# Gated softmax and linear attention on one core: rounds ordered by head group first, and gate logits in 512-column matmuls

## The chip, the core and the metric

The kernel runs on one core of a Trainium2 chip. The metric is the device time of one execution in microseconds (us), as a median of several. A core has five engines that run side by side and meet through semaphores: TensorE (PE; its weight loads are listed as PEld), VectorE (DVE), ScalarE (ACT), GpSimd (POOL) and SyncE (SP), which issues transfers. Matrix products land in PSUM, which has eight banks of 128x512 float32; the other tiles lie in SBUF.

## What is computed

Two attention blocks read the same x, and a sigmoid gate mixes them. Cut to what matters:

```python
B, S, D, H = 1, 2048, 512, 32        # Dh = 16
g = sigmoid((x * gate_w).sum(-1, keepdims=True))
# A: softmax attention
q, k, v = split(x @ A_wqkv)           # 32 heads of 16
p = softmax(q @ k.T * Dh ** -0.5)     # 32 x 2048 x 2048
a = merge(p @ v) @ A_wo
# B: linear attention
q, k, v = split(x @ B_wqkv)
pq, pk = phi(q), phi(k)               # phi(t) = (t + 1 if t > 0 else exp(t)) + 1e-6
o = (pq @ (pk.T @ v)) / (pq @ pk.sum(0) + 1e-6)
b = merge(o) @ B_wo
out = g * a + (1 - g) * b             # bfloat16
```

The softmax part is the large one: 134 million exponentials.

## The kernel before

The program does not write its instructions down in a loop. When it is built, a scheduler in Python plays the engines' clocks with a table of costs, picks at each step the piece of work that could run next, and appends it to that engine's list. On the chip each engine then goes through its fixed list in order and waits on semaphores.

**Rounds.** The attention is cut into 32 rounds. A round has one query block of 512 (`qc`), one group of eight heads (`t8`) and one half of it, four heads (`par`). It has 16 key blocks of 128 with four heads each, so 64 tiles of 128x512 scores.

```python
NR = NQC * 8
def rinfo(r):
    qc, k = divmod(r, 8)
    return qc, k // 2, k % 2          # query block, head group, half
```

**Exp on ACT.** Three or two score tiles at a time, in PSUM banks 0 to 2 or 3 to 4:

```python
gsets = [(0, 1, 2), (3, 4)]
pe(fns, reads=rd, writes=wr2, waves=1, m="row", cols=128 * len(fns))
op(AC, lambda: nc.scalar.activation(PT[:, slot, 0:512 * n], ps[...], ACT.Exp, scale=SCALE), ...)
```

**Exp on DVE.** To relieve ACT, the scheduler may give whole key blocks of a round to DVE, from key block 15 downwards. They use the two PSUM banks 5 and 6, which the small tasks below share. The scores are moved into an integer tile (L1151), from which four passes (L1174, L1177, L1180, L1183) make three factors that are each multiplied by V:

```python
def d_claim():                        # may DVE take a block now?
    r = apos[0]
    if r >= NR or progress() < D0:    # D0 = .8: not before 0.8 of the first round
        return None
    ...
op(DV, lambda: nc.vector.tensor_scalar(Lb[...], src, S1A, S1B, op0=ALU.mult, op1=ALU.add), ...)    # L1151, 1 or 2 tiles
# chain: X = L & 0x7F | 0x3F00; E = L & 0xFF80; X = X * L; L = L + shift
```

P times V is added up for the current round in PSUM bank 7, then transposed by DVE into U (L998), and two rounds (a pair) are normalised into OT, with the gate in the factor.

**Small tasks.** Each takes bank 5 or 6, has matmuls and then an eviction on DVE, and has an earliest progress (`nb`, in rounds) and a due one:

```python
for tb in range(NTB):
    add(("V1", tb), t_v1(tb), V1D + 0.05 * (15 - tb), V1N + V1S * (15 - tb), pre=XT)   # V1D=.7, V1N=.3, V1S=.05
add(("gate",), t_gate(), GD, GN, pre=XT)                                               # GD=1.9, GN=1.5
# K of head group t8: group 1 around 0.3 to 1.3, then
add(("K", t8, t), t_kproj(t8, t), 2 * t8 - 0.9 + 0.1 * t, 2 * t8 - 1.8 + 0.2 * t, pre=XT)
add(("Q", qc, t8), t_qproj(qc, t8), due, due - 0.6, pre=XT)                            # one for two rounds
# phi(K) from 2.5 on, G from 13.2, phi(Q), den, num from 17.2 on,
add(("out", qc, q), t_out(qc, q), ..., max(17.2 + 3.0 * qc + 3.0, 8 * qc + 8.1) + 0.3 * q if qc < 3 else 31.9, ...)
```

**The gate.** All logits come from 64 matmuls of 128 columns into one bank, then sigmoid, and then 16 small copies put it into the layout that the normalisation wants:

```python
for tb in range(NTB):
    pe([mm(BK[b][:, tb:tb + 128], xT[:, cc, 128 * tb:128 * (tb + 1)], gwb[:, cc, :], ...) for cc in range(NCC)], ...)
op(AC, lambda: nc.scalar.activation(eg[:], BK[b][:, 0:NTB], ACT.Exp, scale=-1.0), ...)
...                                    # 1 + e, reciprocal, product
for j in range(4):
    for a in range(4):
        op(DV, lambda j=j, a=a: nc.vector.tensor_copy(gv[32 * j:32 * j + 32, :, a], g0[32 * a:32 * a + 32, :]), ..., cost=0.08)
```

**Fillers.** Where PE would stand, the scheduler puts in matmuls of zeros (`sb_warm`), so that PE's activity stays up.

Of the kernel before, what the change touches and what calls it, by code (L numbers as in the profile page):

```python
# [8 lines left out]
ALU = mybir.AluOpType  # L9
# [136 lines left out]
def bass_gated_mix__mha_block__linear_attn_block__prompt_kernel(  # L146
# [26 lines left out]
    with ExitStack() as es:  # L173
# [23 lines left out]
        OT = SB("OT", [128, 3, 4, 512], BF16)  # L197
# [16 lines left out]
        eg = SB("eg", [128, NTB], FP32)  # L214
        g0 = SB("g0", [128, NTB], FP32)
# [12 lines left out]
        OBT = phk[:, 0:4096].rearrange("p (s i n) -> p s i n", s=2, i=4)  # L228
# [36 lines left out]
        r_OT = [[R(f"OT{s}_{a}") for a in range(4)] for s in range(3)]  # L265
# [8 lines left out]
        r_OBT = [[R(f"OBT{s}_{b}") for b in range(4)] for s in range(2)]  # L274
# [9 lines left out]
        r_g0 = R("g0")  # L284
# [193 lines left out]
        def t_qproj(qc, t8):  # L478
            n = 4 * qc + t8
            s, st = n % 3, n % 2  # L480
            if n == 0:
                lhs, wr = (lambda cc: wA0[:, 1, cc, :]), r_wA0[1]
            else:
                lhs, wr = (lambda cc: wA[:, 0, cc, 128 * t8:128 * (t8 + 1)]), r_wA[0]
            b = yield "bank"
            yield from proj_steps(b, lhs, lambda cc: xT[:, cc, 512 * qc:512 * (qc + 1)], [r_xT[c][qc] for c in range(NCC)] + [wr])
            if n == 0:
                yield ("dve", [r_bk[b], r_maskp], [])
                for p in range(2):
                    op(DV, lambda p=p: nc.vector.tensor_scalar(QP[:, s, p, :], BK[b], maskp[:, p:p + 1], None, op0=ALU.mult),  # L490
                       reads=[r_bk[b], r_maskp], writes=[r_QP[s][p]], cost=0.69)
                yield "free"
                return
            yield ("dve", [r_bk[b]], [r_QT[st]])
            op(DV, lambda: nc.vector.tensor_copy(QT[:, st, :], BK[b]), reads=[r_bk[b]], writes=[r_QT[st]], cost=0.69)
            yield "free"
            for p in range(2):
                for j in range(4):
                    lo = 32 * j + 16 * p
                    dma(QP[lo:lo + 16, s, p, :], QT[lo:lo + 16, st, :], f"qp{s}_{p}", reads=[r_QT[st]],  # L500
                        writes=[r_QP[s][p]] if j == 0 else [], lat=2.5)
                r_QP[s][p].w = _Raw(dma_sems[f"qp{s}_{p}"][0], dma_sems[f"qp{s}_{p}"][1], SP.clock + 2.5)
                r_QP[s][p].r = {}
# [23 lines left out]
        def t_gate():  # L527
            b = yield "bank"
            for tb in range(NTB):
                yield ("pe", xt_all + [r_gwb], [r_bk[b]] if tb == 0 else [], 1.0)  # L530
                pe([mm(BK[b][:, tb:tb + 128], xT[:, cc, 128 * tb:128 * (tb + 1)], gwb[:, cc, :], start=(cc == 0), stop=(cc == NCC - 1))
                    for cc in range(NCC)], reads=xt_all + [r_gwb], writes=[r_bk[b]], waves=1.1, cols=512)
            op(AC, lambda: nc.scalar.activation(eg[:], BK[b][:, 0:NTB], ACT.Exp, scale=-1.0), reads=[r_bk[b]], writes=[r_eg], cost=0.2)
            yield "free"
            yield ("dve", [r_eg], [])
            op(DV, lambda: nc.vector.tensor_single_scalar(g1[:], eg[:], 1.0, ALU.add), reads=[r_eg], writes=[r_g1], cost=0.08)
            op(DV, lambda: nc.vector.reciprocal(g0[:], g1[:]), reads=[r_g1], writes=[r_g0], cost=0.2)
            op(DV, lambda: nc.vector.tensor_tensor(g1[:], eg[:], g0[:], ALU.mult), reads=[r_g0, r_eg], writes=[r_g1], cost=0.1)
            gv = gT[:].rearrange("p (t a) -> p t a", a=4)
            for j in range(4):  # L540
                for a in range(4):
                    op(DV, lambda j=j, a=a: nc.vector.tensor_copy(gv[32 * j:32 * j + 32, :, a], g0[32 * a:32 * a + 32, :]),  # L542
                       reads=[r_g0], writes=[r_gT], cost=0.08)
# [39 lines left out]
        def t_z():  # L583
            b = yield "bank"
            for i in range(4):
                for h in range(4):
                    yield ("pe", r_phiK + [r_const], [r_bk[b]] if i == 0 and h == 0 else [], 1.0)
                    pe([mm(BK[b][:, i:i + 128], phiK[:, tb, 128 * i:128 * (i + 1)], ones[:], start=(tb == 0), stop=(tb == NTB - 1))
                        for tb in range(4 * h, 4 * h + 4)], reads=r_phiK + [r_const], writes=[r_bk[b]], waves=1.1, cols=512)
            yield ("dve", [r_bk[b]], [])  # L590
            op(DV, lambda: nc.vector.tensor_copy(zsb[:], BK[b][:, 0:4]), reads=[r_bk[b]], writes=[r_z], cost=0.17)
            yield "free"
            for i in range(4):
                op(PO, lambda i=i: nc.gpsimd.tensor_scalar(Zsel[:, 8 * i:8 * i + 8], mask8[:], zsb[:, i:i + 1], None, op0=ALU.mult),
                   reads=[r_z, r_mask], writes=[r_Zsel], cost=0.2)
# [41 lines left out]
        def t_num(qc, q):  # L637
# [11 lines left out]
            yield "free"  # L649
            for i in range(4):  # L650
                raw = dma(OBT[:, s, i, 128 * q:128 * (q + 1)], OB[:, sl, 128 * i:128 * (i + 1)], f"obt{sl}",
                          reads=[r_OB[sl]], writes=[r_OBT[s][q]] + r_phiK[0:8] if i == 0 else [], transpose=True, lat=2.5 + i)
            r_OBT[s][q].w = _Raw(dma_sems[f"obt{sl}"][0], dma_sems[f"obt{sl}"][1], raw.t)
            r_OBT[s][q].r = {}
            for x in r_phiK[0:8]:
                x.w = r_OBT[s][q].w

        def t_out(qc, q):
            s = qc % 2
            so = qc % 3  # L660
# [3 lines left out]
            ops_ = [(OBT[:, s, i, 128 * q:128 * (q + 1)], woB[:, i, :], [r_OBT[s][q]]) for i in range(4)]  # L664
            ops_ += [(OT[:, so, a, 128 * q:128 * (q + 1)], woA[:, a, :], [r_OT[so][a]]) for a in range(4)]
            for h in range(4):
                last = qc == NQC - 1 and h == 3
                for kk in ([[6], [7]] if last else [[2 * h, 2 * h + 1]]):
                    if kk == [7]:
                        yield ("wait", ("pair", 8 * qc + 7))  # L670
# [29 lines left out]
        D0 = .8  # L700
        DR0 = 1
# [104 lines left out]
        def rinfo(r):  # L806
            qc, k = divmod(r, 8)
            return qc, k // 2, k % 2
# [25 lines left out]
        def kq_aps(r, kb, j):  # L834
            qc, t8, par = rinfo(r)
            s = (4 * qc + t8) % 3
            return (KT[32 * j:32 * j + 32, t8, 128 * kb:128 * (kb + 1)], QP[32 * j:32 * j + 32, s, par, :],
                    [r_KT[t8][kb // 4], r_QP[s][par]])
# [154 lines left out]
        def round_end(r):  # L993
            qc, t8, par = rinfo(r)
            so = qc % 3
# [9 lines left out]
        def t_norm(qc, t8):  # L1005
            so = qc % 3
# [210 lines left out]
        V1D = .7  # L1217
        V1N = .3
        V1S = .05
        K1D = .6  # L1220
        MH2 = .9
        GD = 1.9
        GN = 1.5
# [7 lines left out]
        for tb in range(NTB):  # L1231
            add(("V1", tb), t_v1(tb), V1D + 0.05 * (15 - tb), V1N + V1S * (15 - tb), pre=XT)
        add(("gate",), t_gate(), GD, GN, pre=XT)
        for t8 in range(1, 4):
            for t in range(4):
                if t8 == 1:
                    due = K1D + (0, 0.5, 0.7, 0.1)[t]
                    add(("K", t8, t), t_kproj(t8, t), due, due - 0.3, pre=XT)
                    continue
                add(("K", t8, t), t_kproj(t8, t), 2 * t8 - 0.9 + 0.1 * t, 2 * t8 - 1.8 + 0.2 * t,  # L1240
                    pre=XT)
        for q4 in range(1, 16):
            qc, t8 = divmod(q4, 4)
            due = K1D + 0.05 if q4 == 1 else 2 * q4 - 0.9
            add(("Q", qc, t8), t_qproj(qc, t8), due, due - 0.6, pre=XT)
        for tb in range(NTB):
            add(("phiK", tb), t_phik(tb), 100 + tb, 2.5 + 0.65 * tb, pre=XT)
        PK = [("phiK", tb) for tb in range(NTB)]
        add(("wq",), t_wq(), 116, 13, pre=PK)
        add(("z",), t_z(), 117, 13, pre=PK)  # L1250
        for k, cc in enumerate((2, 3, 0, 1)):
            add(("G", cc), t_g(cc), 118 + k, 13.2 + 0.8 * k, pre=PK + ([("G", 3)] if cc < 2 else [("G", 2)] if cc == 3 else []))
        GA = [("G", c) for c in range(4)]
        add(("wo",), t_wo(), 123, 16.6, pre=GA + [("z",)])
        add(("kv",), t_kv(), 124, 16.6, pre=GA)
        for qc in range(NQC):
            for i in range(4):
                add(("phiQ", qc, i), t_phiq(qc, i), 130 + 20 * qc + i, 17.2 + 3.0 * qc + 0.5 * i,
                    pre=[("wq",)] + GA + [("num", qc - 2, q) for q in range(4) if qc >= 2])
            add(("den", qc), t_den(qc), 135 + 20 * qc, 17.2 + 3.0 * qc + 2.0,  # L1260
                pre=[("phiQ", qc, i) for i in range(4)] + [("z",), ("gate",)] + [("num", qc - 1, q) for q in range(4) if qc])
            for q in range(4):
                add(("num", qc, q), t_num(qc, q), 136 + 20 * qc + q, 17.2 + 3.0 * qc + 2.1 + 0.2 * q,
                    pre=[("den", qc), ("kv",), ("K", 3, 3), ("z",)] + ([("out", qc - 2, q)] if qc >= 2 else []))
            for q in range(4):
                add(("out", qc, q), t_out(qc, q), 140 + 20 * qc + q, max(17.2 + 3.0 * qc + 3.0, 8 * qc + 8.1) + 0.3 * q if qc < 3 else 31.9,
                    pre=[("num", qc, q), ("wo",)] + ([("pair", 8 * qc + 7)] if qc < 3 else []))
# [142 lines left out]
```

The softmax here doesn't subtract the row's maximum and nothing guards it: scores larger than these inputs give would overflow.

## Time and profile before

| what | value |
|---|---|
| time, median of 3 runs | 784.76 us (782.08 to 785.05) |
| span of the profiled execution | 781.7 us |
| mean clock granted to TensorE | 0.989 |
| chain that ended last | ACT 75%, PE 15%, DVE 6%, issue 3% |
| exp of the scores on ACT (L908) | 653 instructions |
| exp blocks given to DVE (L1174) | 104 of 512 |
| evictions L1151 | 129 of two tiles, 158 of one |
| phi exp on ACT (L550) | 32, mean 772 ns |
| DVE L1151 waiting for PE | 36.5 us in 60 waits |
| ACT L908 waiting for PE | 12.5 us in 10 waits, longest 5.8 |

A page line of instruction groups names the source line, engine and operation, then what it writes and reads with shapes and the count; after the bar, busy us and the mean length of one in ns; after the next bar, the engine's idle time just before them and what ended it. Most matmuls carry L371, because one helper emits them. PE's busy time contains fillers, and matmuls are pipelined, so a busy PE need not be at its peak. The span has a start of 9.66 us before the first exp of scores and ends 8.9 us after the last one.

### The profile page before, as it was taken

Reading aid. Unit: us, or ns where it says so; the run is one execution under the profiler, and the core shown is the slowest. Engines: PE = TensorE matmul, PEld = TensorE weight load, DVE = VectorE, ACT = ScalarE, POOL = GpSimd, SP = SyncE. Lnnn points to the kernel's source line nnn. Section 1 sums busy time; section 2 is a strip of 40 time slices with the busy share of each in tenths; the row PEclk is TensorE's granted clock in tenths of the full one; section 3 lists DMA queues with packets and bytes.
Section 4 is the critical chain, followed back from the end, with each engine's and each line's share of the span. In section 5 each row is a group of like instructions: output and inputs, shape, how many; then the busy total and the mean of one; then the engine's idle time right before and its main releaser. Section 6 shows DMA issues by size and latency. Waiting matters only on the chain.

```text
span 781.7 us, 18175 instructions
## 1 busy us (share of the span) xinstructions
PE 734.5 (94%) x7889; PEld 224.8 (29%) x7950; DVE 703.9 (90%) x997; ACT 758.6 (97%) x690; POOL 9.7 (1%) x36
## 2 busy tenths in 40 slices
PE   8999899999999999999999999999999999999997
PEld 3332322222222222332223223222322322233222
DVE  4498889899999999989999999989999998899995
ACT  5999889999999999999999999999999999999996
POOL 4000000000000000000000000000000000000000
PEclk9999889999999999999999999999999999999999
DMA  7200000000000000102002000110010011001000
GB/s 182 77 7 1 1 8 1 8 1 9 2 5 5 2 8 1 36 2 59 4 1 62 2 8 9 20 37 2 18 28 18 9 22 34 8 12 24 4 2 28
DMA packets 31343, 14.95 MB, mean 19 GB/s; under 512 B 19104, under 2 KB 31264, under 8 KB 31264
## 3 DMA queue, kind: packets, MB, share of 16 engines
q1 hardware_dynamic: 29392, 13.00, 6.4%
q8 instruction: 63, 1.03, 0.6%
q10 hardware_dynamic: 1872, 0.79, 0.4%
q14 instruction: 16, 0.13, 0.1%
HBM read 6.55 MB, written 2.10 MB: 11 GB/s over the span
## 4 chain that ended last, share of the span: by engine, by line
ACT 75%; PE 15%; DVE 6%; issue 3%; DVEq 0%; POOL 0%; ACTq 0%; POOLq 0%
ACT sb_PT L908 73%; PE ps L371 15%; DVE sb_Lb L1151 2%; ACT sb_ebuf L550 2%; DVE sb_Xb L1180 1%; DVE sb_Xb L1174 1%; DVE sb_Eb L1177 0%; DVE sb_Lb L1183 0%; DVE sb_xnat L554 0%; DVE sb_gT L542 0%; DVE sb_OT L1017 0%; DVE sb_Tn L1013 0%; DVE sb_U L998 0%; DVE sb_KT L474 0%; ACT sb_wA L676 0%
## 5 line engine op out<-in xcount | busy, mean ns | idle before, releaser
L908 ACT ACTIVATE sb_PT<-ps 128x1536 bf16<-128x1536 f32 (+1 forms) x653 | 749.7, 1401 | 13.0 <-PE ps L371 12.5
L371 PE MATMUL ps<-sb_QP,sb_KT 32*128 32x512 bf16 x2048 | 308.4, 387 | 28.3 <-ACT sb_PT L908 14.1
L1151 DVE TENSOR_SCALAR sb_Lb<-ps 128x512 uint16<-128x512 f32 (+1 forms) x287 | 264.9, 924 | 38.3 <-PE ps L371 36.5
L371 PE MATMUL ps<-sb_warm 128*17 128x512 bf16 (+7 forms) x2139 | 200.6, 340 | 1.6 <-POOL sb_warm L409 1.3
L371 PEld LDWEIGHTS ps<-sb_QP,sb_KT 32*128 32x128 bf16 x2048 | 77.2, 91 | 284.7 <-ACT sb_PT L908 212.5
L371 PE MATMUL ps<-sb_PT,sb_V 128*17 128x512 bf16 x1632 | 155.9, 387 | 0.9 <-DVE sb_U L998 0.7
L1180 DVE TENSOR_TENSOR sb_Xb<-sb_Xb,sb_Lb 128x2048 bf16<-128x2048 bf16 x104 | 126.5, 1216 | 0.0
L371 PEld LDWEIGHTS ps<-sb_warm 128*17 128x17 bf16 (+2 forms) x2142 | 61.4, 90 | 48.3 <-issue 25.5
L1174 DVE TENSOR_SCALAR sb_Xb<-sb_Lb 128x2048 uint16<-128x2048 uint16 x104 | 71.4, 687 | 1.2
L1177 DVE TENSOR_SCALAR sb_Eb<-sb_Lb 128x2048 uint16<-128x2048 uint16 x104 | 71.2, 684 | 0.0
L1183 DVE TENSOR_SCALAR sb_Lb<-sb_Lb 128x2048 uint16<-128x2048 uint16 x104 | 71.1, 683 | 0.0
L371 PEld LDWEIGHTS ps<-sb_PT,sb_V 128*17 128x17 bf16 x1632 | 37.3, 87 | 99.2 <-issue 90.8
L371 PE MATMUL ps<-sb_Eb,sb_V 128*17 128x512 bf16 x416 | 41.0, 385 | 0.4 <-DVE sb_Eb L1177 0.3
L371 PE MATMUL ps<-sb_Lb,sb_V 128*17 128x512 bf16 x416 | 40.8, 383 | 0.3
L371 PE MATMUL ps<-sb_Xb,sb_V 128*17 128x512 bf16 x416 | 40.8, 383 | 0.1
L371 PE MATMUL ps<-sb_xT,sb_wA 128*128 128x512 bf16 x89 | 28.3, 398 | 3.1 <-issue 2.1
L998 DVE STREAM_TRANSPOSE sb_U<-ps 128x512 f32<-128x512 f32 x32 | 22.7, 708 | 7.5 <-PE ps L371 7.5
L550 ACT ACTIVATE sb_ebuf<-ps 128x512 bf16<-128x512 f32 x32 | 24.7, 772 | 0.0
L371 PE MATMUL ps<-sb_xT,sb_wBx 128*128 128x512 bf16 x54 | 17.2, 396 | 2.2 <-issue 1.1
L371 PE MATMUL ps<-sb_wA,sb_xT 128*128 128x128 bf16 (+1 forms) x128 | 19.0, 275 | 0.2
L371 PE MATMUL ps<-sb_phiK 128*128 128x512 bf16 x55 | 16.9, 382 | 1.4 <-issue 1.3
L474 DVE CAST sb_KT<-ps 128x512 bf16<-128x512 f32 x16 | 11.0, 685 | 8.1 <-PE ps L371 8.1
(80 smaller groups left out, 304.5 us busy)
## 6 DMA issues: line engine op xcount, KB each, us to landing
sb_QP<-sb_QT SPq DMA_DIRECT2D x120, 16.0 KB, 1.8
out_dram<-sb_wA SPq DMA_DIRECT2D x14, 128.0 KB, 1.7
sb_wA<-in_A_wqkv_dram SPq DMA_DIRECT2D x2, 512.0 KB, 6.8
sb_wBx<-in_B_wqkv_dram SPq DMA_DIRECT2D x2, 512.0 KB, 6.1
sb_xnat<-in_A_x_dram SPq DMA_DIRECT2D x2, 512.0 KB, 4.0
sb_phiK<-sb_wA SPq DMA_TRANSPOSE x64, 2.4
sb_xnat<-in_A_x_dram SPq DMA_DIRECT2D x3, 256.0 KB, 3.0
sb_wBv<-in_B_wqkv_dram SPq DMA_DIRECT2D x1, 512.0 KB, 8.9
```

What stands on the lines that cost most here:

```text
L371: return lambda: nc.tensor.matmul(o, lhsT=l, rhs=r, start=start, stop=stop, skip_group_check=sg)
L474: op(DV, lambda: nc.vector.tensor_copy(KT[:, t8, 512 * t:512 * (t + 1)], BK[b]), reads=[r_bk[b]], writes=[r_KT[t8][t]], cost=0.69)
L550: op(AC, lambda: nc.scalar.activation(ebuf[:, s, :], BK[b], ACT.Exp), reads=[r_bk[b]], writes=[r_e[s]], cost=0.48)
L908: op(AC, lambda: nc.scalar.activation(PT[:, slot, 0:512 * n], ps[:, 512 * set_[0]:512 * (set_[0] + n)], ACT.Exp, scale=SCALE), reads=wr, w ...
L998: op(DV, lambda: nc.vector.transpose(U[:, par, :], acc), reads=[r_acc], writes=[r_U[par]], cost=0.71)
L1151: op(DV, lambda: nc.vector.tensor_scalar(Lb[:, sl, 512 * k:512 * (k + n)], src, S1A, S1B, op0=ALU.mult, op1=ALU.add), reads=[r_bk[b] for b ...
L1174: op(DV, lambda: nc.vector.tensor_scalar(X, L, 0x7F, 0x3F00, op0=ALU.bitwise_and, op1=ALU.bitwise_or), reads=[rl], writes=[rx], cost=CH[0])
L1177: ev = op(DV, lambda: nc.vector.tensor_scalar(E_, L, 0xFF80, None, op0=ALU.bitwise_and), reads=[rl], writes=[re_], cost=CH[1])
L1180: ev = op(DV, lambda: nc.vector.tensor_tensor(xb, xb, lb, ALU.mult), reads=[rx, rl], writes=[rx], cost=CH[2])
L1183: ev = op(DV, lambda: nc.vector.tensor_scalar(L, L, float(EXP_SH), None, op0=ALU.add), reads=[rl], writes=[rl], cost=CH[3])
```

## The change

Rounds are ordered by head group first and query block second, so that K, V and Q of the later head groups are needed, and made, much later; small tasks are spread accordingly. Outputs of all query blocks now need the last head group, so all four OT slots are kept and OBT gets four buffers (two of them tiles that are free by then). The gate logits come from 512-column matmuls, one bank task for each 512 rows, with a DVE transpose that brings them into columns; the sum of phi(K) (z) is made in the same way. Exp blocks on DVE may start at progress 1 rather than 0.8. The core of the diff:

```diff
-        OT = SB("OT", [128, 3, 4, 512], BF16)
+        OT = SB("OT", [128, 4, 4, 512], BF16)
-        OBT = phk[:, 0:4096].rearrange("p (s i n) -> p s i n", s=2, i=4)
+        OBT = [phk[:, 0:2048]..., phk[:, 2048:4096]..., wBv[:], GT[:]]
 ...
         def t_gate():
-            b = yield "bank"
-            for tb in range(NTB):
-                ...  # 64 matmuls of 128 columns, one exp, 1 + e, reciprocal, product, 16 copies
+            for t in range(NQC):
+                b = yield "bank"
+                yield from proj_steps(b, lambda cc: gwb[:, cc, :], lambda cc: xT[:, cc, 512 * t:512 * (t + 1)], rd)
+                yield ("dve", [r_bk[b]], [])
+                op(DV, lambda b=b: nc.vector.transpose(rowt[:], BK[b]), ..., cost=0.71)
+                op(DV, lambda t=t: nc.vector.tensor_copy(gl[:, 16 * t:16 * (t + 1)], rowt[...][:, :, 0]), ..., cost=0.17)
+                yield "free"
+            op(AC, lambda: nc.scalar.activation(eg[:], gl[:], ACT.Exp, scale=-1.0), ..., cost=0.2)
+            # 1 + e (0.17), reciprocal of 128x64 (0.6), product (0.2), then
+            for a in range(4):
+                op(DV, lambda a=a: nc.vector.tensor_copy(g1[32 * a:32 * a + 32, :], gv[32 * a:32 * a + 32, :, a]), ..., cost=0.16)
 ...
         def t_z():
-            ...  # 64 matmuls of 128 columns, one copy of 128x4
+            for h in range(8):
+                pe([mm(BK[b], ones[:], phiK[:, tb, :], ...) for tb in (2 * h, 2 * h + 1)], ..., waves=2)
+            op(DV, lambda b=b: nc.vector.transpose(rowt[:], BK[b]), ..., cost=0.71)
+            ...  # four copies, cost 0.16 each
 ...
-        D0 = .8
-        DR0 = 1
+        D0 = 1
+        DR0 = 0
 ...
         def rinfo(r):
-            qc, k = divmod(r, 8)
-            return qc, k // 2, k % 2
+            t8, k = divmod(r, 8)
+            return k // 2, t8, k % 2
 ...
-        V1D = .7
-        V1N = .3
-        V1S = .05
-        K1D = .6
+        V1D = 3
+        V1N = 1.5
+        V1S = .25
+        KN = 6
+        BS = 2.4
-        GD = 1.9
-        GN = 1.5
+        GD = 1.6
+        GN = .9
 ...
-            add(("V1", tb), t_v1(tb), V1D + 0.05 * (15 - tb), V1N + V1S * (15 - tb), pre=XT)
+            k = 15 - tb if tb > 11 else 4 + tb
+            add(("V1", tb), t_v1(tb), V1D + V1S * k, V1N + V1S * k, pre=XT)
 ...
+            for k, t in enumerate((3, 0, 1, 2)):
+                due = 8 * t8 - 1.2 + 0.25 * k
+                add(("K", t8, t), t_kproj(t8, t), due, KN * t8 + 0.4 * k, pre=XT)
 ...
-                add(("out", qc, q), t_out(qc, q), ..., max(17.2 + 3.0 * qc + 3.0, 8 * qc + 8.1) + 0.3 * q if qc < 3 else 31.9,
-                    pre=[("num", qc, q), ("wo",)] + ([("pair", 8 * qc + 7)] if qc < 3 else []))
+                add(("out", qc, q), t_out(qc, q), ..., 26.05 + 2 * qc + 0.35 * q if qc < 3 else 31.9,
+                    pre=[("num", qc, q), ("wo",)] + [("V1", tb) for tb in range(NTB)] + ([("pair", 25 + 2 * qc)] if qc < 3 else []))
```

## The prediction

> **What bounds the kernel now.** I read the page's busy times first, then the busy time of each engine in stages, then the order of instructions around the worst stage, then the groups of instructions.
>
> The busy row of the page:
>
> ```profile
> PE 734.5 (94%) x7889; PEld 224.8 (29%) x7950; DVE 703.9 (90%) x997; ACT 758.6 (97%) x690; POOL 9.7 (1%) x36
> ```
>
> ScalarE (ACT) is busy 758.6 of 781.7 us, so 23.1 us is all that waiting costs on the busiest engine. To find where it lies I cut the span by events: the first softmax exp starts at 9.66, the last ends at 772.77. Columns: stage, its length, then busy us and count on PE, PEld, DVE, ACT, POOL, then granted clock, DMA share, GB/s.
>
> ```profile
> 0.00:9.66 9.66, 7.61 (x41) 3.15 (x41) 3.89 (x10) 1.49 (x3) 7.51 (x30) 1.00 0.79 163
> 9.66:39.00 29.34, 27.35 (x271) 10.73 (x275) 13.07 (x23) 29.12 (x26) 1.05 (x3) 1.00 0.41 119
> 39.00:88.00 49.00, 47.82 (x456) 17.09 (x458) 43.29 (x72) 48.27 (x44) 0.00 (x0) 1.00 0.01 3
> 88.00:104.00 16.00, 13.32 (x89) 2.87 (x91) 12.91 (x32) 11.32 (x10) 0.00 (x0) 0.68 0.01 2
> 104.00:444.00 340.00, 324.06 (x3621) 96.56 (x3648) 321.18 (x437) 340.00 (x313) 1.17 (x4) 1.00 0.04 12
> 444.00:476.00 32.00, 28.82 (x303) 7.78 (x302) 28.49 (x41) 30.69 (x30) 0.00 (x0) 0.89 0.02 6
> 476.00:762.00 286.00, 270.89 (x3010) 82.06 (x3024) 270.65 (x374) 285.80 (x261) 0.00 (x0) 1.00 0.07 17
> 772.77:781.70 8.93, 4.18 (x21) 1.50 (x20) 3.96 (x7) 1.17 (x2) 0.00 (x0) 0.97 0.17 59
> ```
>
> From the first exp to the last, ACT is idle 0.22 + 0.73 + 4.68 + 0 + 1.31 + 0.20 = 7.14 us; the stage from 762 to 772.77, not shown, has none. Two thirds of it is one place, 88 to 104, where the clock fell to 0.68. The rest is 8.2 us at the start and 7.8 us in the tail (8.93 - 1.17). What happens at 88, in order of time:
>
> ```profile
> 87.62 0.17 DVE L538 TENSOR_TENSOR sb_g<-sb_eg,sb_g 128x16 f32<-128x16 f32 x1
> 87.71 3.24 DVE L542 COPY sb_gT<-sb_g 32x16 f32<-32x16 f32 x16
> ...
> 90.99 0.69 DVE L1151 TENSOR_SCALAR sb_Lb<-ps 128x512 uint16<-128x512 f32 x1
> ...
> 91.83 0.61 PE L371 MATMUL ps<-sb_QP,sb_KT 32*128 32x512 bf16 x4 [1.90 <-DVE sb_Lb L1151]
> ...
> 92.49 2.53 ACT L908 ACTIVATE sb_PT<-ps 128x1536 bf16<-128x1536 f32 x2 [1.86 <-PE ps L371]
> ```
>
> The 16 little gate copies hold VectorE (DVE) for 3.24 us. The eviction behind them frees a PSUM bank late; TensorE (PE), which takes its instructions in order, stands for 1.90 us; ACT then stands for 1.86. In four-microsecond stages the clock afterwards is 0.50 from 92 to 100 and 0.77 from 100 to 104; a score matmul lasts 0.61 instead of 0.39 us. PE cannot feed ACT at that clock, and the other 2.8 us (4.68 - 1.86) are lost. The program's own cost table put 0.08 us on each copy, and they took 0.174.
>
> The second limit is the division of the exp work. Of 512 blocks (32 rounds of 16 key blocks, four 128x512 tiles each) ACT does 408 and DVE 104:
>
> ```profile
> L908 ACT ACTIVATE sb_PT<-ps 128x1536 bf16<-128x1536 f32 x326 | 525.2, 1611 | 12.2 <-PE ps L371 12.0
> L908 ACT ACTIVATE sb_PT<-ps 128x1024 bf16<-128x1024 f32 x327 | 389.6, 1192 | 0.8 <-PE ps L371 0.5
> L1151 DVE TENSOR_SCALAR sb_Lb<-ps 128x1024 uint16<-128x1024 f32 x129 | 157.0, 1217 | 9.2 <-PE ps L371 7.9
> L1180 DVE TENSOR_TENSOR sb_Xb<-sb_Xb,sb_Lb 128x2048 bf16<-128x2048 bf16 x104 | 126.5, 1216 | 0.0
> L1151 DVE TENSOR_SCALAR sb_Lb<-ps 128x512 uint16<-128x512 f32 x158 | 107.9, 685 | 29.1 <-PE ps L371 28.6
> ```
>
> On ACT, 72 groups (180 tiles) ran in 81.39 us without a break, so a tile costs 0.452 us and a block 1.81 us. On DVE a block is 157.0 + 107.9 + 126.5 and three passes of 71.4, 71.2 and 71.1, 605.1 us over 104, or 5.8 us; back to back its instructions start some 0.08 us before the last has ended, so about 5.4 us of the engine. Thus 5.4 us of DVE time gained or lost is worth 1.8 us, and only through the number of blocks that the builder can give to DVE.
>
> **What the Trainium skill says.** "TensorE: Matmul & The Clock Gate", section "Part 1: The HAM clock gate", says that the array falls to half clock after an idle window of about 3.4 us and returns after a busy one. The trace agrees on the half clock (0.50), but here PE was not idle for a whole window: it was busy 1.94 of the 4 us from 88, longest gap 1.90. The same page, "Back-to-back issue gap", gives about 216 ns for a warm 512-column matmul; the four-matmul column groups here follow each other every 0.22 us (86.84 to 87.06 to 87.28). "VectorE: DVE Perf Modes", "The TRN2 errata", says that a small DVE instruction is mostly a fixed cost. It agrees: a 32x16 copy takes 174 ns, a 128x512 cast 682. "Perfetto Trace Analysis", "Identifying the Most-Contended Engine", says to rank ScalarE and VectorE by occupancy and not to trust matmul busy time; hence I treat ACT as the bound and not PE's 94%, which contains filler matmuls.
>
> **The change part by part.**
>
> Order of rounds. The 32 rounds, their exp tiles, P times V and normalisations are the same; K (16 casts), V (4 + 16), Q (16), phi and output tasks keep their number. Removed exp work: none. What moves is when evictions come. Before, V1 (16 tasks) and the four K tasks of head group 1 all become eligible between progress 0.3 and about 1.3; K of groups 2 and 3 follow by round 6. After, V1 runs over rounds 1.5 to 5.5 at four per round and K comes at 6, 12 and 18. The crowd at 33 to 90 us thins out. The waits there are little, though: ACT is idle 0.73 us from 39 to 88. I give this 0.5 us.
>
> Gate. PE: 64 matmuls of 128 columns become 16 of 512, the same columns. The 64 have 4.6 us of busy time, 16 at 0.22 to 0.32 are 3.5 to 5: nothing. DVE: before, 0.17 + 0.25 + 0.17 + 3.24 (3.24 as an unbroken run) = 3.8. After, four transposes (the trace has 128x512 f32 at 0.71) and four picks (0.17) spread over four bank tasks, 3.5; then add 0.17, a 128x64 reciprocal (between 0.338 at 32 columns and 0.953 at 128: 0.54), a product 0.2 and four copies at 0.17: 1.6. Total 5.1, so 1.3 us more DVE time, but the unbroken run ahead of a waiting bank falls from 3.8 to 1.6 us, and the new code's cost entries (0.16 to 0.6) agree with these durations. I expect the 88 to 104 hole to go: 4.2 of its 4.68 us.
>
> z sum. The copy of 0.15 becomes a transpose of 0.71 and four of about 0.16: 1.2 us more DVE. With the gate 2.5 us, half a block: 0.8 us more on ACT. PE saves at most 1 us, which is off the path.
>
> First DVE block. The builder's threshold for DVE blocks goes from 0.8 to 1.0 of a round, some 33.4 to 39 us. That leaves about 5 us of DVE unused, up to one block, 1.6 us. Against it, from 39 to 120 DVE is now idle about 11 us (18.2 between 24 and 120, some 7 of it before 39). In later stages it is idle about 1.3 per 24 us; with the crowd gone, 5 to 7 us should come back: 1 block, 1.8 us. These cancel. I leave the count at 104, give or take 3.
>
> Buffers. A fourth OT slot and four OBT buffers remove waits of late phi and output tasks on older ones; no such wait is visible on ACT (0.20 idle in 476 to 762), so 0. Outputs of the first three query blocks move to rounds 26 to 31; the last still waits for the last pair, so start (9.66) and tail (8.9) stay.
>
> Sum: -4.2 (hole) - 0.5 (crowd) + 0.8 (extra DVE work) + 0 (start threshold against crowd) = -3.9. From the 784.8 median: 780.9. The spread of the before runs (782.1 to 785.1) and my belief that a thinner early stage helps block count rather than hurts make me round to 780.
>
> **The rivals.** First: new holes. PE executes a fixed order made from a cost table; three clock dips happened before (92 to 104, 445 to 451, 469 to 475, the last two worth 1.31 us together). V1 at four per round plus phi(K) from round 2.5 is about six bank tasks per round for three rounds, against four later. A dip of the size at 88 costs 4 to 5 us; two of them would give 785 to 790. For: dips follow a PE gap of under 2 us. Against: the long stage 104 to 444 has phi(K), K and G without any loss.
>
> Second: DVE takes more blocks. DVE is idle 54 us between 24 and 768; if the thinner stage let six more blocks through, ACT loses 11 us and the time is about 770. Against: 36 of those 54 us lie after 120, in short waits for PE on L1151, which the change does not treat.
>
> Third: bank pressure lowers the count. Tasks and DVE blocks share two PSUM banks; each held bank turns a 1024-wide eviction (1.217) into two of 0.685. Four gate tasks and late outputs could cost three blocks: 786.
>
> **Range and chances.** Block count, plus or minus 3 (5.4 us), and one dip more or less (4 us) combine to about 6.5 us: 772 to 788, eight in ten. Two per cent is 15.7 us; faster by that needs every hole closed and five extra blocks at once, slower needs four dips or eight lost blocks.
>
> **What would show it.** Right: no stage near 80 to 100 with a clock under 0.9, ACT idle between first and last exp about 3 us, the L1174 count at 101 to 107, first exp near 9.7, tail near 9. Wrong: a count outside that band (block rivals), or new stretches of clock 0.5 in rounds 2 to 6 or where outputs are made (first rival). A longer tail would refute the step on buffers.

## Result and profile after

The kernel after takes 777.40 us (median of 4 runs, 777.24 to 778.97), the kernel before 783.75 us on the same chip (4 runs): ratio 0.9925, 95% interval 0.9898 to 0.9951. The prediction was 780, with 772 to 788 as its range. The busy row of the page after:

```profile
PE 736.3 (95%) x7845; PEld 222.0 (29%) x7905; DVE 701.6 (90%) x978; ACT 758.7 (98%) x692; POOL 10.7 (1%) x36
```

ACT's busy time is the same as before (758.6), in a span that is 4.5 us shorter (777.2 for 781.7). The stages after, in the columns used before (busy us and count on PE, PEld, DVE, ACT, POOL, then clock, DMA share, GB/s); the first exp now starts at 11.47 and the last ends at 767.86:

```profile
0.00:11.47 11.47, 9.30 (x41) 3.77 (x41) 3.88 (x10) 1.49 (x2) 7.94 (x31) 1.00 0.75 155
11.47:38.00 26.53, 24.34 (x255) 10.01 (x258) 8.91 (x16) 26.31 (x24) 0.61 (x1) 1.00 0.41 124
38.00:62.00 24.00, 23.38 (x257) 6.52 (x257) 22.01 (x38) 23.87 (x23) 0.00 (x0) 1.00 0.02 5
62.00:104.00 42.00, 40.76 (x434) 12.16 (x428) 39.80 (x57) 42.00 (x40) 0.00 (x0) 1.00 0.02 4
444.00:476.00 32.00, 30.96 (x353) 9.66 (x352) 31.20 (x43) 32.00 (x30) 0.00 (x0) 1.00 0.02 6
767.86:777.20 9.34, 5.77 (x28) 2.23 (x27) 3.95 (x7) 1.18 (x3) 0.00 (x0) 1.00 0.17 56
```

Between first and last exp ACT is idle 0.37 us, before 7.15. The clock is 1.00 in every stage. The account of the two profiles: start 9.66 to 11.47 (+1.81), from first to last exp 763.11 to 756.39 (-6.72), tail 8.93 to 9.34 (+0.41), together -4.5. The start is no property of the change: the profiles of experiments 1 and 2 have the late first exp (11.4) with the start of the kernel before, that of experiment 5 the early one (9.45) with the start of the kernel after. Without it the account gives -6.3, which is the difference of the medians.

The gate's final chain in the kernel after, in order of time (start, length, engine, line):

```profile
45.66 0.28 ACT L539 ACTIVATE sb_eg<-sb_gl 128x64 f32<-128x64 f32 x1
...
46.20 0.18 DVE L541 TENSOR_SCALAR sb_gl<-sb_eg 128x64 f32<-128x64 f32 x1
46.41 0.55 DVE L542 RECIPROCAL sb_gT<-sb_gl 128x64 f32<-128x64 f32 x1
...
47.00 0.22 DVE L543 TENSOR_TENSOR sb_gl<-sb_eg,sb_gT 128x64 f32<-128x64 f32 x1
...
47.26 0.76 DVE L546 COPY sb_g<-sb_gl 32x16 f32<-32x16 f32 x4
```

It holds DVE for 1.8 us, at 46 to 48 us, long before the first normalisation (68.55), and PE works through it. The groups by shape show the exp work:

```profile
L915 ACT ACTIVATE sb_PT<-ps 128x1536 bf16<-128x1536 f32 x327 | 538.4, 1647 | 8.0 <-PE ps L373 7.9
L1187 DVE TENSOR_TENSOR sb_Xb<-sb_Xb,sb_Lb 128x2048 bf16<-128x2048 bf16 x103 | 125.1, 1215 | 0.0
```

DVE has 103 blocks for 104. Of ACT's waits for PE 7.9 us remain, of which 7.6 are the start.

Of the signs that the prediction named, the clock (no stage under 0.9), the count and the tail came as said. ACT's idle time is 0.37 us where about 3 were expected, and the first exp of this profile is late.

### The profile page after: what moved, and what is told of

Read it like the earlier page. It is cut to its first block, busy times and chain, and to the rows that moved or that the text cites. A ratio compares the mean times of both kernels' runs of the same rounds, so it can differ in the third digit from the quotient of the medians.

```text
span 777.2 us, 18041 instructions
## 1 busy us (share of the span) xinstructions
PE 736.3 (95%) x7845; PEld 222.0 (29%) x7905; DVE 701.6 (90%) x978; ACT 758.7 (98%) x692; POOL 10.7 (1%) x36
## 4 chain that ended last, share of the span: by engine, by line
ACT 87%; PE 5%; DVE 4%; issue 2%; DMA 1%; DVEq 0%; SPq 0%; ACTq 0%
ACT sb_PT L915 85%; PE ps L373 5%; ACT sb_ebuf L554 2%; DVE sb_Lb L1158 2%; DMA sb_xT<-in_A_x_dram 1%; DVE sb_Xb L1187 0%; DVE sb_Xb L1181 0%; DVE sb_Eb L1184 0%; DVE sb_phiK L558 0%; DVE sb_rowt L535 0%; SPq L306 0%; DVE sb_Lb L1190 0%; DVE sb_KT L476 0%; ACT sb_wA L683 0%; DVE sb_U L1005 0%
## 5 line engine op out<-in xcount | busy, mean ns | idle before, releaser
L915 ACT ACTIVATE sb_PT<-ps 128x1536 bf16<-128x1536 f32 (+1 forms) x655 | 751.3, 1436 | 8.0 <-PE ps L373 7.9
L1158 DVE TENSOR_SCALAR sb_Lb<-ps 128x1024 uint16<-128x1024 f32 (+1 forms) x272 | 260.7, 959 | 36.8 <-PE ps L373 34.0
L373 PE MATMUL ps<-sb_warm 128*17 128x512 bf16 (+9 forms) x2200 | 200.9, 342 | 1.3 <-POOL sb_warm L411 1.3
L554 ACT ACTIVATE sb_ebuf<-ps 128x512 bf16<-128x512 f32 x32 | 26.3, 821 | 0.0
L373 PE MATMUL ps<-sb_phiK,sb_OT 128*128 128x512 bf16 x63 | 18.2, 382 | 0.2 <-issue 0.2
```

The costliest lines, as they stand in the source:

```text
L373: return lambda: nc.tensor.matmul(o, lhsT=l, rhs=r, start=start, stop=stop, skip_group_check=sg)
L554: op(AC, lambda: nc.scalar.activation(ebuf[:, s, :], BK[b], ACT.Exp), reads=[r_bk[b]], writes=[r_e[s]], cost=0.48)
L1158: op(DV, lambda: nc.vector.tensor_scalar(Lb[:, sl, 512 * k:512 * (k + n)], src, S1A, S1B, op0=ALU.mult, op1=ALU.add), reads=[r_bk[b] for b ...
```

## The experiments

Each run is compared with the kernel before in the same session, hence the ratios. In all kernels every output is computed; the form of the gate, order, placement, costs and dates differ. The new form of the z sum and the added buffers were not tried alone. In the kernel after, ACT has no idle time from 104 to 444, where the z sum lies (334.6), and 0.02 us from 476 to 762.

**1. The copies on GpSimd, in the old order.** Two theories: the burst of copies on DVE made the hole, or the crowded order did.

```diff
-                    op(DV, lambda j=j, a=a: nc.vector.tensor_copy(gv[...], g0[...]), ..., cost=0.08)
+                    op(PO, lambda j=j, a=a: nc.gpsimd.tensor_copy(gv[...], g0[...]), ..., cost=0.25)
```

> The kernel before with one edit: the 16 gate copies run on GpSimd instead of VectorE. Order of rounds, dates, matmuls unchanged. Burst theory (the 3.24 us of copies on VectorE made the hole at 88 to 104 us): ACT waits near 90 us vanish, clock there stays 1.0, time 777 to 779.5. Order theory (the crowd of V1 and K tasks in the first rounds is what costs, the copies only mark it): still a hole of 3 us or more between 60 and 120 us, time 782 or more.

Measured: 780.34 for 782.91, ratio 0.9964 (0.9950 to 0.9978). The large hole is gone, but the time stays above the burst theory's band; the profile has idle time elsewhere, and its first exp is late (11.44). Stages of this run:

```profile
76.00:120.00 44.00, 39.91 (x395) 13.52 (x393) 36.96 (x61) 42.91 (x41) 3.85 (x16) 1.00 0.02 4
164.00:192.00 28.00, 26.57 (x296) 7.66 (x296) 26.62 (x38) 27.27 (x25) 0.00 (x0) 0.94 0.03 6
432.00:456.00 24.00, 22.01 (x239) 6.13 (x238) 22.92 (x34) 23.21 (x22) 0.00 (x0) 0.93 0.01 2
696.00:720.00 24.00, 23.02 (x274) 6.89 (x272) 21.75 (x27) 23.05 (x21) 0.00 (x0) 0.93 0.10 22
```

Idle ACT in 76 to 120 is 1.09 us at clock 1.00 (before: 5.2 in 72 to 120, at 0.88 to 0.91). But two dips stand where there was none, 164 to 192 and 696 to 720, and one is where it was, near 445. ACT's idle time from first to last exp is 4.0 us for 7.15. In 88 to 104 alone it is 0.4 us for 4.68.

**2. True costs for the builder, same instructions.**

```diff
-   ... nc.vector.tensor_copy(gv[...], g0[...]), reads=[r_g0], writes=[r_gT], cost=0.08)
+   ... nc.vector.tensor_copy(gv[...], g0[...]), reads=[r_g0], writes=[r_gT], cost=0.2)
    # likewise 1 + e 0.08 to 0.17, reciprocal 0.2 to 0.26, product 0.1 to 0.18
```

> The kernel before with one edit: the builder's costs of the gate's VectorE chain are set to what the trace shows (copies 0.20 with their gap, for 0.08; 0.17, 0.26, 0.18 for the other three). The same instructions are executed, in an order made for the true durations. If the hole came from the wrong table, the order adapts and the time is 778 to 780.5. If it is the unbroken VectorE run itself, the hole at 88 to 104 stays at 3 us or more and the time is 782 to 785. Order theory: 782 to 785 too.

Measured: 779.91, ratio 0.9954 (0.9941 to 0.9967): the first band. The copies still take 3.25 us of DVE in one run, but the builder now puts PE work that needs no DVE beside them. ACT loses 2.8 us in 72 to 120 for 5.2 (2.2 in 88 to 104 for 4.68), and the clock there falls to 0.58 for one stage of 4 us instead of 0.50 for two:

```profile
96.00:100.00 4.00, 3.83 (x22) 0.73 (x22) 3.29 (x7) 2.55 (x3) 0.00 (x0) 0.58 0.05 12
```

So about half of the hole came from wrong entries in a table, not from the instructions.

**3. The old gate in the new order.** The edit puts the old gate task, with its 16 copies at cost 0.08, into the kernel after.

> The kernel after with its gate task put back to the old one (64 matmuls of 128 columns into one bank, 16 copies with cost 0.08); rounds stay in the new order. Burst theory: a hole with a clock dip comes back behind the copies, 4 to 6 us, time 781 to 784. Order theory: the thin early stage swallows the burst, time 776.5 to 778.5, no dip.

Measured: 780.37, ratio 0.9966 (0.9954 to 0.9978), some 3 us above the kernel after (the ratios differ by 0.0041): just under the burst theory's band, and clearly out of the other's. In order of time:

```profile
43.69 3.23 DVE L546 COPY sb_gT<-sb_g 32x16 f32<-32x16 f32 x16
44.13 0.39 PE L375 MATMUL ps<-sb_QP,sb_KT 32*128 32x512 bf16 x4
46.95 0.72 DVE L1005 STREAM_TRANSPOSE sb_U<-ps 128x512 f32<-128x512 f32 x1
...
47.73 0.60 PE L375 MATMUL ps<-sb_PT,sb_V 128*17 128x512 bf16 x4 [3.20 <-DVE sb_U L1005]
...
48.93 2.54 ACT L915 ACTIVATE sb_PT<-ps 128x1536 bf16<-128x1536 f32 x2 [2.68 <-PE ps L375]
```

The thin early stage doesn't swallow the burst. Here the transpose of U is behind the copies, PE's next P times V needs the bank that U empties, and PE, which goes in order, stands for 3.20 us. Its clock is 0.50 from 48 to 52, and the matmuls last 0.60 us. From 43 to 56 ACT loses 3.97 us; in the rest of the exp stage 0.25.

**4. The new gate in the old order.** The edit puts the new gate task into the kernel before, with the dates of before.

> The kernel before with the new gate alone (four bank tasks with 512-column matmuls, transposes, short final chain) in the old order of rounds. Burst theory: the hole is gone, 778 to 780. Order theory: four more bank tasks in the crowded stage make it worse there, one DVE block fewer in round 3 and the time 784 or more.

Measured: 786.05, ratio 1.0037 (1.0024 to 1.0050): slower, by less than half a per cent. The time falls into the order theory's band, but its reason, a block lost, did not come: the count is 104. Two stages of it, then the place of the gate in the first (final chain, first normalisation, transpose of U, PE's wait for it):

```profile
90.00:104.00 14.00, 11.94 (x81) 2.73 (x81) 10.48 (x22) 11.59 (x12) 0.00 (x0) 0.76 0.04 9
336.00:342.00 6.00, 4.92 (x53) 1.57 (x51) 4.54 (x7) 2.02 (x2) 0.66 (x1) 1.00 0.01 3
```

```profile
90.04 0.20 DVE L541 TENSOR_SCALAR sb_gl<-sb_eg 128x64 f32<-128x64 f32 x1 [0.36 <-ACT sb_eg L539]
...
91.90 0.35 DVE L1014 RECIPROCAL sb_rden<-sb_U 128x32 f32<-128x32 f32 x1
...
93.88 0.67 DVE L1002 STREAM_TRANSPOSE sb_U<-ps 128x512 f32<-128x512 f32 x1
...
94.61 0.60 PE L373 MATMUL ps<-sb_PT,sb_V 128*17 128x512 bf16 x4 [0.98 <-DVE sb_U L1002]
```

In the first, ACT loses 2.41 us, about half of what the kernel before loses in the same place (4.68). The four gate tasks come late there (their transposes start at 80.8 to 88.8 us; 38.1 to 44.7 in the kernel after). The first normalisation needs the gate, and U's two halves are free for the third round only after it. So the final chain (90.04 to 91.9), the normalisation (91.90 to 93.95) and the transpose of U (93.88) follow one another directly; PE waits 0.98 us for that transpose, and the clock dips. In the second, ACT loses 3.98 us at full clock: a G task has twelve matmuls in one unbroken run of 2.76 us ahead of the scores. The tail is 1.9 us longer too (10.80). So a short chain was not enough to close the hole here, and what makes this run slower than the kernel before lies elsewhere: in the order around the G task, whose code the edit leaves as it is, and in the tail.

**5. The gate's dates of before, in the kernel after.**

```diff
-        GD = 1.6
-        GN = .9
+        GD = 1.9
+        GN = 1.5
```

> The kernel after, with the gate's dates of before (due 1.9, earliest 1.5, for 1.6 and 0.9), so that it falls into the start of the V1 tasks and nearer to the first normalisation. If an early gate is what keeps its final chain away from the normalisation and U transpose, a PE wait on U and a clock dip come back near 60 to 80 us and the time is 779.5 to 782. If the short chain is harmless wherever it lies, 776.5 to 778.5.

Measured: 778.73, ratio 0.9945 (0.9926 to 0.9964). No dip came back (clock 1.00 in the profiled run). The profile has 1.06 us of idle ACT for 0.37: in 0.48 of it ACT waits in front of the gate's exp (66.94) for DVE's last logits. The time lies just above the second band, and below the first. These dates cost about 1 us at most; the interval does not separate it from the kernel after. The start and the end of the final chain:

```profile
67.42 0.19 DVE L541 TENSOR_SCALAR sb_gl<-sb_eg 128x64 f32<-128x64 f32 x1
...
68.49 0.76 DVE L546 COPY sb_g<-sb_gl 32x16 f32<-32x16 f32 x4
```

The chain runs straight into the first normalisation (69.28), as in run 4, and nothing happens to the clock: the third transpose of U comes only at 89.13. Task and dates are those of run 4; in the new order of rounds the chain ends 19.9 us before that transpose, in the old one 2.0. So the gate need not be early, nor clear of the normalisation.

**6. The old gate in the new order, copies on GpSimd.** The edits of runs 1 and 3 together.

> The kernel after with the old gate (64 matmuls of 128 columns), but its 16 copies on GpSimd. If the 512-column form is worth nothing on TensorE and only the VectorE burst counted, this equals the kernel after: 776.5 to 778.5. If the wide matmuls themselves save time, 779 or more. Against the kernel before with the same copies on GpSimd (780.3) the difference is what the order of rounds brings without the burst: about 3.

Measured: 779.87, ratio 0.9954 (0.9937 to 0.9972), in the band of the wide matmuls. But near the gate there is nothing; of 1.31 us idle ACT in the profile, 1.06 is a dip at 144 to 168. So the wide matmuls did not bring the difference through PE's work at the gate. What the order of rounds brings once no burst is there is the step from run 1 to this one, 0.9964 to 0.9954: not separated from zero, where 3 us were expected. A part of this run's time lies outside its core's span, for a cause that was not traced: the six executions took 1.8 to 3.7 us more than their spans, those of the kernel after about 1.8. By the median spans (778.5 in run 1, 777.1 here, and 781.1 and 781.4 for the kernel before) the step is about 1.7 us, with spans that overlap.

**7. The start threshold of before, in the kernel after.**

```diff
-        D0 = 1
-        DR0 = 0
+        D0 = .8
+        DR0 = 1
```

> The kernel after with the start threshold of DVE blocks as before (0.8, no block of round 0). Prediction's step: the later start is worth nothing either way, because the count of blocks stays (103): 776.5 to 778.5 and ACT busy time equal. Rival: starting at 34 us instead of 40 gives a block back, 775 to 776.5; or it crowds the gate, 779 or more with a dip near 45.

Measured: 778.45, ratio 0.9938 (0.9920 to 0.9956), 103 blocks, exp stage 756.73 us for 756.39. The threshold is worth nothing that can be seen; the median is at the edge of the band because of the start. The runs fall into two groups, 777.60, 777.62, 777.69 and 779.21, 779.21, 779.32.

**8. Three warm-up matmuls more at the start.** The first K and Q projections in the kernel before, the kernel after and this run (start, length, eight matmuls of 512 columns):

```profile
6.49 1.89 PE L371 MATMUL ps<-sb_xT,sb_OT 128*128 128x512 bf16 x8 [0.71 <-DVE sb_xT L462]
```

```profile
6.61 3.57 PE L373 MATMUL ps<-sb_xT,sb_OT 128*128 128x512 bf16 x8 [0.84 <-DMA sb_xT<-in_A_x_dram]
```

```profile
6.56 1.89 PE L373 MATMUL ps<-sb_xT,sb_OT 128*128 128x512 bf16 x8 [0.77 <-DMA sb_xT<-in_A_x_dram]
```

```diff
         need(("xtr", 0))
+        pe([mm(BK[k % 5], warm[:, 0:128], warm) for k in range(3)], reads=[r_warm], writes=r_bk[0:3], waves=3)
         need(("K", 0, 0))
```

> The kernel after with three more matmuls of zeros on PE between the first x transposes and the first K projection, to keep PE active while it waits for x. Start theory (runs of one kernel differ by about 1.8 us because the first eight projections run at 0.21 or at 0.43 us each, depending on where PE's idle time before them falls): first exp always near 9.7 us, spread of runs under 1 us, median 776 to 777. Otherwise the spread and the median stay as in the kernel after (777.2 to 779).

Measured: 777.33, ratio 0.9925 (0.9908 to 0.9942); five of six runs lie between 776.89 and 777.45, the sixth at 778.33 with a clock of 0.997. The first exp is at 9.73. Median and spread (1.44 us) miss what the start theory asked for; its explanation of the jump is borne out all the same. The eight matmuls took 3.57 us in the kernel after and 1.89 in run 5, whose start is the same code, and the first exp came at 11.47 and 9.45: the jump is TensorE's pace at the start. That three more matmuls prevent it is likely, since the two groups of run 7 are gone, but six runs don't show it. They bring nothing to the median (ratio 0.9925 with and without), since most runs of the kernel after were of the quick group; the exp stage (756.39 us) is exactly that of the kernel after.

**9. 105 blocks on DVE.** Run 8 with a start threshold of 0.75 and other small settings:

```diff
-        DFAR = 0.8
-        D0 = 1
-        DR0 = 0
-        RES = .2
-        V1S = .25
-        PKS = 0.65
-        GN = .9
+        DFAR = 1.2
+        D0 = .75
+        DR0 = 1
+        RES = .3
+        V1S = .2
+        PKS = 0.6
+        GN = .8
```

> The kernel after with the three warm-up matmuls of the last run and with builder settings (start threshold 0.75, look-ahead and dates slightly moved) under which it gives 105 blocks to DVE for 103, with no work left out. If a block moved to DVE is worth its 1.81 us of ACT time, 3.6 us less than the run with warm-up matmuls (777.3): 773 to 775. If the moved blocks are paid back in new PE gaps and clock dips, 776.5 to 780 with ACT idle over 2 us between first and last exp.

Measured: 773.82 (773.73 to 774.61), ratio 0.9877 (0.9857 to 0.9896): faster than the kernel before by 1.2%, and its interval lies just below that of the kernel after. The stage from first to last exp, in this run and then in run 8:

```profile
9.97:762.93 752.96, 717.10 (x7765) 215.70 (x7825) 703.95 (x983) 752.55 (x684) 4.46 (x6) 1.00 0.06 17
```

```profile
9.73:766.12 756.39, 721.76 (x7785) 216.19 (x7845) 693.96 (x962) 756.02 (x688) 3.17 (x7) 1.00 0.06 17
```

DVE works 10.0 us more and ACT 3.47 us less: 1.74 us of ACT for a block, where the prediction had 1.81, for 5.0 us of DVE, where it had 5.4. ACT is idle 0.41 us. Seven settings moved together, and which of them let the two blocks in was not tried.

**10. 104 blocks, one in the first round.** Run 8 with one setting, D0 = 0.7 for 1.

> The kernel after with the three warm-up matmuls and one setting moved (start threshold 0.7 for 1), under which one block of the first round goes to DVE, 104 in all. One block less on ACT: 1.8 us under 777.3, that is 775 to 776. If the early start crowds the gate tasks at 38 to 48 us: 777.5 or more, with idle ACT there.

Measured: 778.02, ratio 0.9926 (0.9910 to 0.9943). The block is there, and what it saved is lost in 2.65 us of idle ACT: 1.24 in 48 to 72, later than the rival had it, and 0.94 in 192 to 216, where the clock is 0.93. One setting changes the order far behind it, too.

## Why the prediction was right, and where it missed

The mechanism was right: nothing of the work that binds ACT became less, and the gain is idle time of ACT. The sum was -3.9 from 784.8, rounded to 780; measured are -6.35 from 783.75. By the profiles it is -4.68 for the hole, -0.60 for the crowd, -1.49 for the later stages, +0.06 of work on ACT and +0.41 in the tail, -6.3 together. The rounding from 780.9 to 780 was for a better block count; the count fell by one, so that part of the nearness is luck.

- **Hole, -4.2.** It went (42 us at 1.00, ACT busy all of them). That the burst of copies costs about 3 us is shown both ways: out of the old order -2.6 (run 1), into the new order about +3 (run 3). No profile in the new order, other than run 3's, has a clock dip between the first exp and 140 us. The prediction gave the whole credit to the shorter chain. Run 4 leaves it about half: in the old order the new gate still loses 2.41 of 4.68 us at this place. The other half came with the new order. Read from runs 4 and 5, it is the time between the gate's final chain and the third transpose of U, 2.0 us in the one and 19.9 in the other; an edit of this distance alone was not made.
- **Crowd, -0.5.** From 38 to 62 ACT is idle 0.13 us, before 0.73 from 39 to 88. The size fits; runs 1 and 6 say no more than that it is small.
- **Later dips, left out of the sum and so taken as fixed.** This step failed. The 1.31 us at 444 to 476 are gone too, with 0.18 of the 0.20 in 476 to 762, and no new dip came. The first rival, new holes, was the right question with the sign reversed: runs 1, 6 and 10 each have dips in places of their own, and the kernel after has none (clock 1.0 in all four runs). Of the eight profiles in the new order two have one between 140 us and the last exp (runs 6 and 10), of the four in the old order three (the kernel before and runs 1 and 2). That is a hint that the new order favours it, and no more. Why each dip comes where it does was not traced, and this quarter of the gain stays open.
- **Extra DVE work, +0.8.** The chain is 1.8 us for 1.6 predicted, and one block is lost (103), inside the band. By its price that is 1.8 us of ACT, yet ACT's busy time from first to last exp is 756.02 for 755.96. The group of exp grew by 1.6 us (749.7 to 751.3), as four more tiles should, and the other instructions of ACT overlap more with it. That fewer breaks leave more such overlap is argued from this, not measured by itself.
- **Start and tail, 0.** Tail +0.41. The start jumps by 1.7 us between runs of one kernel, which the prediction did not see; the spread of before (782.1 to 785.1) has room for it.
- **Start threshold against crowd, 0.** Run 7: 0. DVE was idle 12.0 us from 24 to 48 (before 7.7), about as predicted, and starting earlier does not bring the lost block back.
- **Second rival, more blocks.** It did not happen in this change. Run 9 shows that it was open all the same: two blocks more for 3.5 us.
- **Third rival, bank pressure.** It did not come: 140 evictions are of two tiles and 132 of one, before 129 and 158.

## What to carry to other kernels

Where a program's order is fixed ahead by a cost table, compare the table with the trace before anything else. Sixteen small copies entered at 0.08 us took 0.17 and a gap each, about 2 us more than planned in all; ACT lost 4.68 us, because PE stood behind them and then ran at half clock, and right entries alone brought 3.0 us (run 2). Test a part alone as well as the whole, and see where the idle time of such a test lies before you judge the part: the new gate in the old order halved its hole and lost the gain elsewhere. Ask also what must wait for a late task, here the third transpose of U for the gate, and how much time stands between them. When the bound engine has no idle time left, move work off it (here 1.74 us a block), and check the new order's clock before believing the sum.

## What the runs showed of the hardware

- After a PE gap of 1.90 us (kernel before) the mean clock was 0.50 from 92 to 100 and 0.77 from 100 to 104; around one of 3.20 us (run 3) it was 0.80, 0.50 and 0.84 in three stages of 4 us from 44 on. The Trainium skill, "TensorE: Matmul & The Clock Gate", section "Part 1: The HAM clock gate", speaks of an idle window of about 3.4 us; here each gap was shorter than that, with little work beside it (PE busy 1.94 us in 88 to 92, and 0.80 in 44 to 48 of run 3). How little is enough does not come out: PE busy 2.58 us of 92 to 96 in run 1 left the clock at 1.00, and 2.88 us of 444 to 448 in the kernel before went with 0.83, behind a gap of 1.12 us.
- The clock column reads 1.00 in the first 11.47 us of the kernel after, while eight matmuls of 512 columns take 3.57 us there (1.89 in the kernel before and in run 5). Near the start the lengths of matmuls say more than the clock column.
- A copy of 32x16 took 0.174 us on DVE and 0.206 on GpSimd (median of sixteen in run 1, the longest 0.748; times on GpSimd are rough).
